# Attention then a feed-forward layer on one core: one ring of four PSUM banks, and a pair's steps dealt out anew

## The chip, the cores and the metric

One core of a Trainium2 chip runs the whole program. The core has a matrix engine (TensorE, rows PE; its weight loads PEld), VectorE (DVE), ScalarE (ACT), GpSimd (POOL), and SyncE (SP), which here issues the DMAs. Matmul results go to PSUM, eight banks of 128 partitions by 512 fp32 values. The metric is the device time of one execution in microseconds (us); the kernel before has a median of 1268.96 us over 3 runs (1266.4 to 1271.8).

## What is computed

Block-causal attention over 8 batches of 8 heads, 576 positions of width 64, in blocks of 64; its output, laid out as 4608 tokens of width 512, goes through a feed-forward layer (FFN) of inner width 2048:

```python
scores = (1 / sqrt(64)) * q @ k.T                  # per batch and head, 576 x 576
scores = where(block_i >= block_j, scores, -1e9)   # blocks of 64
attn   = softmax(scores)
x      = (attn @ v).transpose(0, 2, 1, 3).reshape(4608, 512)
h = x @ w_in                                       # 512 -> 2048
g = where(h >= 1, h, where(h <= -1, 0, (h + 1) ** 2 / 4))
out = g @ w_out                                    # 2048 -> 512
```

## The kernel before

**Pairs and steps.** Two heads of one batch make a pair; there are 32 pairs, run one after the other by `attention_steps`, a generator that hands out eight steps for each pair (called steps 0 to 7 below; a step ends at a `yield`). `cur` is the pair at work, `old` the one before it, `nxt` the one after. Batches from 2 on (pairs 8 to 31, flags `far` and `raw`) run their steps in one pattern, which is called the body below. `scores(j, g)` multiplies q and k of head j for one or two row tiles, reduces the maximum (DVE L505), takes exp (ACT L509, with a read of the accumulated sum behind it), and scales (DVE L491, L492, L515); a DMA then moves the result to another tile (prr). `turn(j, g)` transposes it on PE into a PSUM bank and `split` copies it out in a high part (ACT L545) and a low part (DVE L547). `turn_last` does the same for the last 64 rows of both heads, whose last 64 x 64 pieces, the corner, go by a fifth transposition to a bank and to the tiles pcs. `attn_v_first` multiplies the first 256 rows of both heads with v (8 matmuls, tiles pa), `attn_v(j)` the other 320 rows of one head (10 matmuls, tiles pb and pcs); `add_halves` adds the two halves (ACT L613 to xtmp, DVE L614 to x), and `store_x` makes x ready for the FFN. `turned_raw` (q and k of one head, four transpositions, L401) and `turned_last` (their last blocks, one transposition, L442) prepare the next pair: two copies on ACT (L388, L394) and two on DVE (L389, L395) that take turns on one bank, and in `turned_last` two more on DVE (L446).

**FFN.** `feed_forward` walks 9 chunks of 512 tokens and 16 slices of the inner width: `ffn_in` is 12 matmuls of 512 columns (L770, tile ph), then ACT L779, DVE L780, DVE L783, ACT L784 and POOL L785; `ffn_out` is 12 matmuls (L794, L799). From step 36 of the program on (pair 4) each step of attention is followed by one of them: in the body `ffn_in` follows steps 1, 3, 5, 7 and `ffn_out` steps 0, 2, 4, 6. What the FFN has left when attention ends, about 68 of its 288 pieces, runs alone.

**What sets the order.** The code is handed to a scheduler that orders each engine's instructions by the order in which they are written, but takes a later one first where its own clock says that an earlier one cannot start; it also gives each PSUM tile its bank. The engines then work through these fixed orders. A bank can be written again when its last reader is done, so a tile in a ring of three waits for the third or fourth one before it.

**Banks.** Before, attention has three banks (`ps_w`), `ffn_in` one of its own (`ps_h`), and `ffn_out` four (`ps_o`, lent to attention until the FFN starts):

```python
def work_bank(name):
    banks["n"] += 1
    if banks["free"] and banks["n"] % 2:
        return ps_o.tile([P, 512], F32, tag="po", name=name)
    return ps_w.tile([P, 512], F32, tag="work", name=name)
```

Of the kernel before, what the change touches and what calls it, by code (L numbers as in the profile page):

```python
# [23 lines left out]
def block_attn_then_ffn(  # L24
# [13 lines left out]
    P = 128  # L38
# [34 lines left out]
    dram = ctx.enter_context(tc.tile_pool(name="dram", bufs=1, space=bass.MemoryType.DRAM))  # L73
    ps_w = ctx.enter_context(tc.tile_pool(name="ps_w", bufs=3, space=bass.MemoryType.PSUM))
    ps_h = ctx.enter_context(tc.tile_pool(name="ps_h", bufs=1, space=bass.MemoryType.PSUM))
    ps_o = ctx.enter_context(tc.tile_pool(name="ps_o", bufs=NTT, space=bass.MemoryType.PSUM))

    banks = {"free": True, "n": 0}

    def work_bank(name):  # L80

        banks["n"] += 1
        if banks["free"] and banks["n"] % 2:
            return ps_o.tile([P, 512], F32, tag="po", name=name)
        return ps_w.tile([P, 512], F32, tag="work", name=name)
# [169 lines left out]
    class Pair:  # L255
# [238 lines left out]
        def scores(self, j, g):  # L494
            tiles = self.GROUPS[g]
            m = len(tiles)
            ps = work_bank("ps_s")
            pr = att3.tile([P, S], F32, tag="pr", name="pr")
            nm = small.tile([P, 2], F32, tag="nm", name="nm")
            sm = small.tile([P, 2], F32, tag="sm", name="sm")  # L500
            cols = [slice(at, at + (t + 1) * P) for t, at in tiles]
            for (t, _), cs in zip(tiles, cols):
                self.product(ps[:, cs], j, t * P, 0, (t + 1) * P, True, True)
            for i, cs in enumerate(cols):
                nc.vector.tensor_reduce(  # L505
                    out=nm[:, i : i + 1], in_=ps[:, cs], axis=AX.X, op=ALU.max, negate=True
                )
            for i, cs in enumerate(cols):
                nc.scalar.activation(  # L509
                    pr[:, cs], ps[:, cs], AF.Exp, bias=nm[:, i : i + 1], scale=1.0,  # L510
                    accum_out=sm[:, i : i + 1],
                )
            self.inverse(sm[:, :m])
            for i, cs in enumerate(cols):
                nc.vector.tensor_scalar_mul(pr[:, cs], pr[:, cs], sm[:, i : i + 1])  # L515
            self.pr[j, g] = as_float32r(pr[:, : cols[-1].stop], self.plain) if self.hop else [pr]

        def scores_last(self):
# [22 lines left out]
            nc.vector.tensor_scalar_mul(pr, pr, sm[:, 2:3])  # L541
            self.pr["last"] = as_float32r(pr, self.plain) if self.hop else [pr]

# [12 lines left out]
        def turn(self, j, g):  # L556
# [4 lines left out]
            for c0 in range(0, n, P):  # L561
                self.transposed(ps[:, c0 : c0 + P], pr, c0, P)
            if g == 0:
                self.split(ps[:, :n], *self.pa[j])
# [7 lines left out]
        def turn_last(self):  # L572
            pr = self.pr.pop("last")
            ps = work_bank("ps_t")
            for c0 in range(0, SM, P):
# [4 lines left out]
            )  # L580
            ps = work_bank("ps_t")
            self.transposed(ps[:BLK, :P], pr, SM, BLK)
            self.split(
                ps[:BLK, :P].rearrange("p (h c) -> p h c", h=2), *(x[:BLK] for x in self.pc)
            )

# [20 lines left out]

        def add_halves(self, ps, j, c0):
            main = slice(j * D, (j + 1) * D)
            rest = slice((1 - j) * D, (2 - j) * D)  # L610
            n = ps.shape[1]
            xtmp = att1.tile([P, G1], F32, tag="xtmp", name="xtmp")
            nc.scalar.copy(xtmp[main, :n], ps[rest, :])  # L613
# [17 lines left out]
        def attn_v_first(self):  # L631
# [3 lines left out]
            for j in range(2):  # L635
                self.weighted(ps[:, j * G0 : (j + 1) * G0], j, self.parts_first(j))
            for j in range(2):
                self.add_halves(ps[:, j * G0 : (j + 1) * G0], j, 0)

        def attn_v(self, j):  # L640
# [3 lines left out]
            self.weighted(ps, j, self.parts(j))  # L644
            self.add_halves(ps, j, G0)

# [16 lines left out]
    def attention_steps():  # L663
# [10 lines left out]
        for i, cur in enumerate(pairs + [None]):  # L674
# [9 lines left out]
            if far:  # L684
                old.attn_v_first()
            if near:
# [4 lines left out]
            if cur:  # L691
                cur.scores(0, 1)
                cur.turned_last()
            if i + 2 < len(pairs):
                pairs[i + 2].fetch()
            if near:
                old.attn_v(1)
                old.store_x()
            yield
            if far:  # L700
                old.attn_v(1)
                old.store_x()
            if not cur:
                return
            if cur.far:
                cur.scores(0, 2)
            else:
                cur.begin()
                cur.scores(0, 2)
                cur.turn(0, 0)  # L710
# [35 lines left out]
            else:  # L746
                cur.scores(1, 2)
                cur.attn_v(0)
                cur.turn(1, 0)
            yield  # L750
            if cur.far:
                cur.turn(1, 0)
                cur.attn_v(0)
            else:
                cur.turn(1, 1)
                cur.attn_v_first()
# [6 lines left out]
    def ffn_in(c, fc):  # L763
        at = (c * TCH) % RING
        ph = ps_h.tile([P, 512], F32, tag="ph", name="ph")
        fs = slice(fc * P, (fc + 1) * P)
# [118 lines left out]
```

## Time and profile before

| what | value |
|---|---|
| median of 3 runs | 1268.96 us (1266.4 to 1271.8) |
| the profiled execution: time | 1269.69 us |
| the profiled execution: span from first to last instruction | 1267.9 us |
| PE busy | 1200.1 us (95%) |
| DVE / ACT / POOL busy | 887.0 / 703.2 / 394.6 us |
| granted TensorE clock, mean | 0.981 |
| attention alone, weights prepared beside it | about the first 140 us |
| attention and FFN together | to about 1080 us |
| FFN alone | from about 1080 us |

A matmul's row gives its modelled end; matmuls overlap, so the distance from one start to the next says more than the length of a row. "[0.38 <-DVE x L614]" behind a row is the engine's idle time before it and what ended that idle time. In the rows of windows the columns are: the stretch, its length, then for PE, PEld, DVE, ACT and POOL the busy time with the count of instructions, then the granted TensorE clock, the share of the DMA engines' time, and GB/s.

### The profile page before, as it was taken

The numbers are of one execution on the slowest core, as the hardware profiler recorded it, in microseconds if no ns is written. First come the engines' busy times: TensorE is split into PE (matmuls) and PEld (weight loads), VectorE is DVE, ScalarE is ACT, GpSimd is POOL, SyncE is SP. The second block draws the span as 40 slices with busy tenths as digits, with TensorE's granted clock in tenths as the row PEclk, the third lists the DMA queues.
The fourth block names the chain that finished last, engine by engine and source line by source line (L and its number), as shares of the span: only waits on it lengthen the run. The fifth ranks groups of instructions, "written<-read, shape, count | busy, mean of one in ns | idle before, by whom it ended". The sixth has DMA issues, their size and how long they took to land.

```text
span 1267.9 us, 20253 instructions
## 1 busy us (share of the span) xinstructions
PE 1200.1 (95%) x6280; PEld 998.8 (79%) x6280; DVE 887.0 (70%) x2188; ACT 703.2 (55%) x1827; POOL 394.6 (31%) x430
## 2 busy tenths in 40 slices
PE   5888889899999999999999999999999999999998
PEld 4666667678888888888888888888888888888886
DVE  8898877758777777777777777787777777322222
ACT  5787656646566655665656655566556555222222
POOL 3555655522222222222222222222222222222222
PEclk9888988999999999999999999999999999999999
DMA  5566666667888655555554655465556433422432
GB/s 158 167 176 215 203 228 197 217 198 237 260 273 266 215 162 158 154 175 163 156 162 145 187 157 152 138 189 153 160 154 190 137 128 118 132 87 98 133 100 100
DMA packets 185259, 215.43 MB, mean 170 GB/s; under 512 B 113840, under 2 KB 132272, under 8 KB 184384
## 3 DMA queue, kind: packets, MB, share of 16 engines
q1 hardware_dynamic: 185152, 214.14, 54.9%
q8 instruction: 50, 0.82, 0.3%
q14 instruction: 57, 0.47, 0.1%
HBM read 134.74 MB, written 31.98 MB: 131 GB/s over the span
## 4 chain that ended last, share of the span: by engine, by line
PE 69%; DVE 16%; ACT 6%; issue 5%; DMA 1%; POOL 1%; SPq 1%; ACTq 0%; POOLq 0%; DVEq 0%
PE ph L770 29%; PE po L794 15%; PE po L799 7%; PE ps_av L591 7%; PE ps_s L482 4%; ACT pr L509 3%; PE ps_s L485 3%; DVE t L780 2%; PE ps_t L552 2%; DVE t L783 2%; ACT t L779 2%; DVE pb L547 2%; DVE nm L505 2%; DVE sm L491 1%; DVE pr L515 1%
## 5 line engine op out<-in xcount | busy, mean ns | idle before, releaser
L785 POOL TENSOR_TENSOR gl<-t,gh 128x512 fp32r<-128x512 f32 x144 | 187.5, 1302 | 510.2 <-ACT gh L784 333.2
L794 PE MATMUL po<-wo,gh 128*128 128x512 f32 x1152 | 296.1, 397 | 0.5 <-DMA wo<-wo_split 0.3
L794 PEld LDWEIGHTS po<-wo,gh 128*128 128x128 f32 x1152 | 212.5, 189 | 44.5 <-DMA wo<-wo_split 0.7
L770 PE MATMUL ph<-xh,wih 128*128 128x512 f32 x576 | 232.9, 404 | 1.6 <-DVE t L783 1.6
L770 PE MATMUL ph<-xh,wil 128*128 128x512 f32 x576 | 228.8, 397 | 0.0
L770 PE MATMUL ph<-xl,wih 128*128 128x512 f32 x576 | 227.8, 396 | 0.5 <-DVE xl L627 0.5
L780 DVE SCALAR_TENSOR_TENSOR t<-t 128x512 f32<-128x512 f32 x144 | 101.5, 705 | 168.0 <-ACT t L779 165.2
L779 ACT ACTIVATE t<-ph 128x512 f32<-128x512 f32 x144 | 85.9, 597 | 173.8 <-PE ph L770 173.8
L509 ACT ACTIVATE pr<-ps_s,nm 128x128 f32<-128x128 f32 (+3 forms) x256 | 134.1, 527 | 60.5 <-DVE nm L505 58.4
L784 ACT CAST gh<-t 128x512 fp32r<-128x512 f32 x144 | 89.5, 621 | 120.3 <-DVE t L783 120.0
L799 PE MATMUL po<-wo,gl 128*128 128x512 f32 x576 | 155.6, 392 | 0.0
L482 PE MATMUL ps_s<-ka,qa 68*128 68x288 f32 (+4 forms) x384 | 135.3, 367 | 15.0 <-ACT pr L509 5.4
L379 POOL TENSOR_TENSOR vsr<-vn,vsr 128x256 fp32r<-128x256 f32 (+1 forms) x96 | 55.2, 576 | 246.2 <-ACT vsr L378 244.6
L770 PEld LDWEIGHTS ph<-xh,wil 128*128 128x128 f32 x576 | 109.5, 190 | 23.8
L770 PEld LDWEIGHTS ph<-xh,wih 128*128 128x128 f32 x576 | 109.8, 191 | 21.7 <-DVE t L783 2.3
L799 PEld LDWEIGHTS po<-wo,gl 128*128 128x128 f32 x576 | 108.7, 189 | 23.1
L505 DVE TENSOR_REDUCE nm<-ps_s 128x1 f32<-128x128 f32 (+3 forms) x256 | 118.8, 482 | 10.4 <-PE ps_s L485 9.4
L770 PEld LDWEIGHTS ph<-xl,wih 128*128 128x128 f32 x576 | 109.7, 190 | 20.5 <-DVE xl L627 0.9
L485 PE MATMUL ps_s<-kb,qb 128*128 128x288 f32 (+4 forms) x384 | 121.1, 322 | 0.0
L515 DVE TENSOR_SCALAR pr<-pr,sm 128x128 f32<-128x128 f32 (+3 forms) x256 | 107.3, 440 | 5.4
L783 DVE TENSOR_TENSOR t<-ph,t 128x512 f32<-128x512 f32 x144 | 98.7, 686 | 2.2
L491 DVE TENSOR_SCALAR sm<-sm 128x1 f32<-128x1 f32 (+1 forms) x224 | 52.0, 232 | 68.3 <-ACT pr L509 65.7
(111 smaller groups left out, 1871.4 us busy)
## 6 DMA issues: line engine op xcount, KB each, us to landing
wo<-wo_split SPq DMA_DIRECT2D x144, 512.0 KB, 3.5
prr<-pr SPq DMA_DIRECT2D x96, 192.0 KB, 2.5
prr<-pr SPq DMA_DIRECT2D x72, 256.0 KB, 2.8
out_dram<-ob SPq DMA_DIRECT2D x36, 256.0 KB, 2.9
bits<-in_moe_w_in_dram SPq DMA_DIRECT2D x32, 256.0 KB, 3.5
bits<-in_moe_w_out_dram SPq DMA_DIRECT2D x32, 256.0 KB, 3.0
wo_split<-ws SPq DMA_DIRECT2D x16, 512.0 KB, 2.9
qa<-qb SPq DMA_DIRECT2D x63, 128.0 KB, 2.4
```

The costliest lines, as they stand in the source:

```text
L482: nc.tensor.matmul(ps, qa[:KA, j, c0 : c0 + P], ka[:KA, j, k0 : k0 + n], start=first, stop=False)
L485: nc.tensor.matmul(ps, qb[:, j, c0 : c0 + P], kb[:, j, k0 : k0 + n], start=False, stop=last)
L505: nc.vector.tensor_reduce(out=nm[:, i : i + 1], in_=ps[:, cs], axis=AX.X, op=ALU.max, negate=True)
L509: nc.scalar.activation(pr[:, cs], ps[:, cs], AF.Exp, bias=nm[:, i : i + 1], scale=1.0, accum_out=sm[:, i : i + 1],)
L515: nc.vector.tensor_scalar_mul(pr[:, cs], pr[:, cs], sm[:, i : i + 1])
L770: nc.tensor.matmul(ph, w[:, cc, fs], x[:, cc, xs], start=(cc == 0 and i == 0), stop=(cc == NCC - 1 and i == 2),)
L779: nc.scalar.activation(t_, ph, AF.Relu, bias=0.5, scale=0.5)
L780: nc.vector.scalar_tensor_tensor(out=t_, in0=t_, scalar=1.0, in1=t_, op0=ALU.min, op1=ALU.mult)
L783: nc.vector.tensor_tensor(out=t_, in0=ph, in1=t_, op=ALU.max)
L785: nc.gpsimd.tensor_tensor(out=gl, in0=t_, in1=gh.bitcast(F32), op=ALU.subtract)
L794: nc.tensor.matmul(po[tt], gh[:, ts_], wo[:, w, :], start=(fc == 0 and w == 0), stop=False)
L799: nc.tensor.matmul(po[tt], gl[:, ts_], wo[:, 0, :], start=False, stop=fc == NFC - 1)
```

## The change

- `ps_h` is gone; `ps_w` has four banks instead of three, and `ffn_in` takes its bank from the same ring as attention.
- In the body `attn_v(0)` of the old pair moves from step 7 to step 0, `attn_v_first` from step 0 to step 1, and `attn_v(1)` in step 2 behind `scores(0, 2)` instead of ahead of it.
- `turned_last` for the next pair moves from its own step 1 to step 6 of the pair ahead of it.
- The corner is no longer transposed in `turn_last` (step 6) into a bank of its own, but in `turn(1, 0)` (step 7) into the unused last quarter of that bank.
- `add_halves` gets its xtmp from its caller; `attn_v_first` uses one for both heads. `moved` only gives a name to a line.

```diff
-    ps_w = ctx.enter_context(tc.tile_pool(name="ps_w", bufs=3, space=bass.MemoryType.PSUM))
-    ps_h = ctx.enter_context(tc.tile_pool(name="ps_h", bufs=1, space=bass.MemoryType.PSUM))
+    ps_w = ctx.enter_context(tc.tile_pool(name="ps_w", bufs=4, space=bass.MemoryType.PSUM))
...
@@ turn
             for c0 in range(0, n, P):
                 self.transposed(ps[:, c0 : c0 + P], pr, c0, P)
+            if self.far and j == 1 and g == 0:
+                self.turn_corner(self.pr.pop(("last",)), ps[:BLK, n : n + P])
...
@@ turn_last
-            ps = work_bank("ps_t")
-            self.transposed(ps[:BLK, :P], pr, SM, BLK)
-            self.split(
-                ps[:BLK, :P].rearrange("p (h c) -> p h c", h=2), *(x[:BLK] for x in self.pc)
-            )
+            if not self.far:
+                self.turn_corner(pr, work_bank("ps_t")[:BLK, :P])
+
+        def turn_corner(self, pr, ps):
+
+            self.transposed(ps, pr, SM, BLK)
+            self.split(ps.rearrange("p (h c) -> p h c", h=2), *(x[:BLK] for x in self.pc))
...
@@ attn_v_first
+            xtmp = att1.tile([P, G1], F32, tag="xtmp", name="xtmp")
             for j in range(2):
-                self.add_halves(ps[:, j * G0 : (j + 1) * G0], j, 0)
+                self.add_halves(ps[:, j * G0 : (j + 1) * G0], j, 0, xtmp)
...
@@ attention_steps, step 0
             if far:
-                old.attn_v_first()
+                old.attn_v(0)
@@ step 1
             if cur:
                 cur.scores(0, 1)
-                cur.turned_last()
+                if not cur.raw:
+                    cur.turned_last()
...
+            if far:
+                old.attn_v_first()
@@ step 2
-            if far:
-                old.attn_v(1)
-                old.store_x()
-            if not cur:
-                return
-            if cur.far:
-                cur.scores(0, 2)
-            else:
-                cur.begin()
-                cur.scores(0, 2)
+            if not cur:
+                old.attn_v(1)
+                old.store_x()
+                return
+            if not cur.far:
+                cur.begin()
+            cur.scores(0, 2)
+            if far:
+                old.attn_v(1)
+                old.store_x()
+            if not cur.far:
                 cur.turn(0, 0)
@@ step 6
+            if nxt and nxt.raw:
+                nxt.turned_last()
@@ step 7
             if cur.far:
                 cur.turn(1, 0)
-                cur.attn_v(0)
@@ ffn_in
-        ph = ps_h.tile([P, 512], F32, tag="ph", name="ph")
+        ph = work_bank("ph")
```

**PE in the body, steps 6 and 7**, from `turn(0, 2)` to the first matmul of `ffn_in`. Before (ps_t: the transposed tiles; ps_s: the scores; po: `ffn_out`; ps_av: attn times v; ps_qk: the next pair's q and k):

```order
L552 MATMUL ps_t<-ident_r,prr 128x128 x4
L552 MATMUL ps_t<-ident_r,prr 64x128
L482 MATMUL ps_s<-ka,qa 128x512
L485 MATMUL ps_s<-kb,qb 128x512
L794 MATMUL po<-wo,gh 128x512 x8
L799 MATMUL po<-wo,gl 128x512 x4
L552 MATMUL ps_t<-ident_r,prr 128x128 x3
```

The ten matmuls of `attn_v(0)` follow here, then four transpositions for ps_qk (L401) and `ffn_in`. The change:

```order
L558 MATMUL ps_t<-ident_r,prr 128x128 x4
L482 MATMUL ps_s<-ka,qa 128x512
L485 MATMUL ps_s<-kb,qb 128x512
L442 MATMUL ps_qk<-ident_r,qk 128x128
L809 MATMUL po<-wo,gh 128x512 x8
L814 MATMUL po<-wo,gl 128x512 x4
L558 MATMUL ps_t<-ident_r,prr 128x128 x3
L558 MATMUL ps_t<-ident_r,prr 64x128
L401 MATMUL ps_qk<-ident_r,qk 128x128 x4
L785 MATMUL ph<-xh,wih 128x512
```

The corner (64x128) moved behind `ffn_out`, the transposition of `turned_last` (L442) came in behind the scores, and between the corner and `ffn_in` only four transpositions are left. In every fourth pair the scheduler puts four of the po matmuls ahead of L442, and three of the next step's po matmuls ahead of that step's transpositions. The bank that this `ffn_in` takes is that of the 512-column scores in the same piece; the bank of the ten matmuls of `attn_v(0)`, now in step 0, is that of the L401 transpositions.

**DVE in the body, steps 6 and 7**, from the reduction of the 512-column scores to L395 of `turned_raw`. Before:

```order
L505 TENSOR_REDUCE nm<-ps_s 128x1
L491 TENSOR_SCALAR sm<-sm 128x1
L492 RECIPROCAL sm<-sm 128x1
L515 TENSOR_SCALAR pr<-pr,sm 128x512
L547 TENSOR_TENSOR pa_8700<-ps_t,pa_8699 128x384
L614 TENSOR_TENSOR x_8703<-ps_av,xtmp 64x320
L389 SCALAR_TENSOR_TENSOR qb<-ps_qk,qb 64x512
L395 TENSOR_TENSOR kb<-ps_qk,kb 64x512
```

The change:

```order
L505 TENSOR_REDUCE nm<-ps_s 128x1
L389 SCALAR_TENSOR_TENSOR qb<-ps_qk,qb 64x2x64
L491 TENSOR_SCALAR sm<-sm 128x1
L395 TENSOR_TENSOR kb<-ps_qk,kb 64x2x64
L492 RECIPROCAL sm<-sm 128x1
L446 TENSOR_SCALAR qa<-ps_qk 64x2x64
L515 TENSOR_SCALAR pr<-pr,sm 128x512
L446 TENSOR_SCALAR ka<-ps_qk 64x2x64
L553 TENSOR_TENSOR pcs_107<-ps_t,pcs_106 64x128
L389 SCALAR_TENSOR_TENSOR qb<-ps_qk,qb 64x512
L553 TENSOR_TENSOR pa_8671<-ps_t,pa_8670 128x384
L395 TENSOR_TENSOR kb<-ps_qk,kb 64x512
```

The four copies of `turned_last` (the 64x2x64 ones) came in between the reduction and the scaling, the corner's low part (pcs) moved from ahead of the reduction to behind it, and the addition of `attn_v(0)` (L614) went to step 0.

**PE early, in pair 1**, around the transpositions for q of the next pair. Before, two of the first `ffn_in`'s twelve matmuls stand here, long before their place in the code (the other ten follow in pairs 1 to 4):

```order
L422 MATMUL ps_qk<-ident_r,qs 128x128 x4
L770 MATMUL ph<-xh,wih 128x512
L770 MATMUL ph<-xl,wih 128x512
L554 MATMUL ps_t<-ident_r,pr 128x128 x4
L482 MATMUL ps_s<-ka,qa 128x384
L485 MATMUL ps_s<-kb,qb 128x384
```

The change:

```order
L422 MATMUL ps_qk<-ident_r,qs 128x128 x4
L560 MATMUL ps_t<-ident_r,pr 128x128 x4
L482 MATMUL ps_s<-ka,qa 128x384
L485 MATMUL ps_s<-kb,qb 128x384
L560 MATMUL ps_t<-ident_r,pr 128x128 x4
L560 MATMUL ps_t<-ident_r,pr 64x128
```

With the bank of its own gone, all twelve matmuls of the first `ffn_in` stand in pair 4, at their place in the code.

More of the change, by code (lines that the diff above doesn't have):

```diff
@@ L515, in scores, with moved @@
                 nc.vector.tensor_scalar_mul(pr[:, cs], pr[:, cs], sm[:, i : i + 1])
-            self.pr[j, g] = as_float32r(pr[:, : cols[-1].stop], self.plain) if self.hop else [pr]
+            self.pr[j, g] = [pr[:, : cols[-1].stop]]
+            self.moved(j, g)
+        def moved(self, *key):
+            if self.hop:
+                self.pr[key] = as_float32r(self.pr[key][0], self.plain)
         def scores_last(self):
@@ L541, in scores_last @@
             nc.vector.tensor_scalar_mul(pr, pr, sm[:, 2:3])
-            self.pr["last"] = as_float32r(pr, self.plain) if self.hop else [pr]
+            self.pr["last",] = [pr]
+            self.moved("last")
         def split(self, ps, hi, lo=None):
@@ L572, in turn_last @@
         def turn_last(self):
-            pr = self.pr.pop("last")
+            pr = self.pr["last",] if self.far else self.pr.pop(("last",))
             ps = work_bank("ps_t")
@@ L606, in parts, with add_halves @@
             return (*parts, (NTL, SM - G0, [x[:, j, :] for x in self.pc]))
-        def add_halves(self, ps, j, c0):
+        def add_halves(self, ps, j, c0, xtmp):
             main = slice(j * D, (j + 1) * D)
@@ L611, in add_halves @@
             n = ps.shape[1]
-            xtmp = att1.tile([P, G1], F32, tag="xtmp", name="xtmp")
             nc.scalar.copy(xtmp[main, :n], ps[rest, :])
@@ L644, in attn_v @@
             self.weighted(ps, j, self.parts(j))
-            self.add_halves(ps, j, G0)
+            self.add_halves(ps, j, G0, att1.tile([P, G1], F32, tag="xtmp", name="xtmp"))
         def store_x(self):
```

## The prediction

> **What bounds the kernel now.** First I read the view of windows, one stretch for each stage (attention with the preparation of weights, the transition, the body, the FFN alone):
>
> ```profile
> 40.00:140.00 100.00, 81.95 (x437) 65.22 (x436) 91.47 (x261) 77.17 (x232) 55.90 (x69) 0.90 0.62 187
> 140.00:280.00 140.00, 123.48 (x570) 95.51 (x568) 99.59 (x246) 79.27 (x221) 68.90 (x84) 0.91 0.67 213
> 280.00:1080.00 800.00, 785.88 (x4353) 665.98 (x4353) 613.70 (x1506) 477.01 (x1227) 210.46 (x219) 1.00 0.58 175
> 1080.00:1268.00 188.00, 182.79 (x807) 150.64 (x805) 49.89 (x73) 44.27 (x74) 43.99 (x34) 0.99 0.33 108
> ```
>
> Up to 140 us VectorE is the busy one (91.5 of 100 us). From 280 us on the matrix engine is: 785.9 of 800 us, at a granted clock of 1.00. The body is all that the new steps touch, and PE's idle time there is 14.1 us. Then the waits of PE in that stretch (engine and line, what it waited for, us in total, times, longest):
>
> ```profile
> PE ps_qk L442 <- DVE x L614: 8.9, 23, 0.4
> PE ps_s L482 <- ACT pr L509: 5.2, 17, 0.3
> ```
>
> These two are the 14.1 us. The first stands in step 1 of 23 pairs: the transposition of `turned_last` wants the bank that `attn_v_first` used, and the second addition is late. The second stands in step 6 of 17 pairs: the 512-column scores want the bank of the 384-column scores of step 5, whose exp is late. Both are one delay: PE is ahead of VectorE and ScalarE, and a ring of three banks passes it on.
>
> The idle time understates them, since a matmul's row runs on while nothing follows. From start to start, in one pair:
>
> ```profile
> 595.08 0.34 PE L485 MATMUL ps_s<-kb,qb 128*128 128x384 f32 x1
> 595.26 0.39 PE L770 MATMUL ph<-xh,wih 128*128 128x512 f32 x1
> ...
> 611.83 0.34 PE L485 MATMUL ps_s<-kb,qb 128*128 128x384 f32 x1
> 612.55 0.25 PE L442 MATMUL ps_qk<-ident_r,qk 128*128 128x128 f32 x1 [0.38 <-DVE x L614]
> 612.64 0.46 PE L770 MATMUL ph<-xh,wih 128*128 128x512 f32 x1
> ```
>
> Where nothing is waited for, the next start comes 0.18 us after the 384-column matmul; here it comes 0.72 us after. The stall is 0.54 us, not 0.38. (The Trainium skill, "Trainium Kernel Development and Optimization", Performance Expectations, says that matmul busy time is a bad metric because matmuls are pipelined; by the busy time the two stalls would be worth 14.1 us, by the starts some 20, and the starts here bear the page out.)
>
> **The stretch in which the pair's second half is decided.** Steps 6, 7 and the next step 0, from the timeline of the same pair:
>
> ```profile
> 597.99 0.51 PE L552 MATMUL ps_t<-ident_r,prr 128*128 128x128 f32 x5
> 598.58 0.19 ACT L509 ACTIVATION_READ_ACCUMULATOR pr<-ps_s,nm 128x1 f32 x1
> 598.82 0.50 PE L482 MATMUL ps_s<-ka,qa 68*128 68x512 f32 x1 [0.33 <-ACT pr L509]
> 599.40 0.39 PE L794 MATMUL po<-wo,gh 128*128 128x512 f32 x1
> 600.73 0.68 DVE L783 TENSOR_TENSOR t<-ph,t 128x512 f32<-128x512 f32 x1
> 601.33 0.27 DVE L547 TENSOR_TENSOR pcs<-ps_t,pcs 64x128 fp32r<-64x128 f32 x1
> 601.52 0.67 DVE L505 TENSOR_REDUCE nm<-ps_s 128x1 f32<-128x512 f32 x1
> 602.14 0.37 PE L552 MATMUL ps_t<-ident_r,prr 128*128 128x128 f32 x3
> 602.28 0.69 ACT L509 ACTIVATE pr<-ps_s,nm 128x512 f32<-128x512 f32 x1 [0.22 <-DVE nm L505]
> 602.35 1.31 PE L591 MATMUL ps_av<-pb,vsr 128*128 128x320 f32 x8
> 602.87 0.19 ACT L509 ACTIVATION_READ_ACCUMULATOR pr<-ps_s,nm 128x1 f32 x1
> 603.09 0.15 DVE L491 TENSOR_SCALAR sm<-sm 128x1 f32<-128x1 f32 x1 [0.90 <-ACT pr L509]
> 603.28 0.16 DVE L492 RECIPROCAL sm<-sm 128x1 f32<-128x1 f32 x1
> 603.48 0.49 DVE L515 TENSOR_SCALAR pr<-pr,sm 128x512 f32<-128x512 f32 x1
> 603.66 0.53 PE L401 MATMUL ps_qk<-ident_r,qk 128*128 128x128 f32 x4
> 603.88 0.55 DVE L547 TENSOR_TENSOR pa<-ps_t,pa 128x384 fp32r<-128x384 f32 x1
> 604.03 0.46 PE L770 MATMUL ph<-xh,wih 128*128 128x512 f32 x1
> 606.87 0.37 PE L552 MATMUL ps_t<-ident_r,prr 128*128 128x128 f32 x3
> 607.08 0.29 PE L482 MATMUL ps_s<-ka,qa 68*128 68x128 f32 x1
> 607.61 1.03 PE L591 MATMUL ps_av<-pa,vsr 128*128 128x256 f32 x8
> ```
>
> Three transpositions take 0.21 us (602.14 to 602.35), so five take 0.35 and the scores could start at 598.34; they start at 598.82, 0.05 after the accumulator's read ends (598.77). That stall is 0.48 us. A pair with both loses 1.02 us.
>
> **What the change does, part by part.** No instruction is added or taken away; every matmul, copy and DMA has its old size. No DMA belongs to a moved step; on SP's queue only the loads of q and k for a later pair begin earlier, after L401 in step 7 instead of after L442 in step 1, and nothing reads them for a pair's time.
>
> *Step 1's stall goes.* L442 leaves step 1. `attn_v_first` comes in there, but with half a step of matmuls and `ffn_in` behind it; the bank of its sums is not asked for again before step 3. Gain 0.54 us a pair.
>
> *Step 6's stall goes.* The 512-column scores take the bank of the transpositions of step 5, whose low copy is long done. L442 now takes the bank of the 384-column scores, free for PE at 598.82. PE comes there at 597.99 + 0.28 (four transpositions) + 0.58 (598.82 to 599.40) = 598.85. Gain 0.48 us, with 0.03 us to spare; if the exp were 0.2 us later, L442 would wait 0.17.
>
> *A stall in step 7 comes.* I follow PE on: L442 takes 0.09 (612.55 to 612.64), to 598.94; `ffn_out` 2.74 (599.40 to 602.14), to 601.68; four transpositions 0.28, to 601.96; L401 0.37 (603.66 to 604.03), to 602.33. The ten matmuls of `attn_v(0)`, 1.31 us long, are no longer in between. There `ffn_in` wants the bank of the 512-column scores. Their reduction is behind DVE L783, which this change leaves where it was; without the corner's copy it starts at 601.33 instead of 601.52 and ends 0.67 later at 602.00. The exp follows after 0.09 (as 602.19 to 602.28) and its accumulator read ends 0.78 after its start (602.28 to 603.06), at 602.87; PE goes on 0.05 later, at 602.92. Stall 0.59 us. Queued behind it: all of `ffn_in`, then step 0.
>
> *A stall in step 0 comes.* PE goes on: `ffn_in` 2.84 (604.03 to 606.87), to 605.76; three transpositions and four matmuls of scores 0.74 (606.87 to 607.61), to 606.50. There `attn_v(0)` now wants the bank of L401, whose last reader is DVE L395. VectorE has the new pieces ahead of it; these rows give them and the pair of L389 and L395:
>
> ```profile
> 605.08 0.69 DVE L389 SCALAR_TENSOR_TENSOR qb<-ps_qk,qb 64x512 fp32r<-64x512 f32 x1 [0.21 <-ACT qb L388]
> 605.80 0.58 ACT L394 CAST kb<-ps_qk 64x512 fp32r<-64x512 f32 x1 [0.75 <-DVE qb L389]
> 606.42 0.69 DVE L395 TENSOR_TENSOR kb<-ps_qk,kb 64x512 fp32r<-64x512 f32 x1 [0.65 <-ACT kb L394]
> ...
> 615.36 0.29 DVE L395 TENSOR_TENSOR kb<-ps_qk,kb 64x128 fp32r<-64x128 f32 x1
> 615.66 0.28 DVE L446 TENSOR_SCALAR qa<-ps_qk 64x128 fp32r<-64x128 f32 x1
> 615.96 0.29 DVE L446 TENSOR_SCALAR ka<-ps_qk 64x128 fp32r<-64x128 f32 x1
> ```
>
> From the accumulator read (602.87) L491 starts at 602.90; by distances from start to start: L491 0.19, L395 of the last blocks 0.30, L492 0.20, L446 0.30, L515 0.40 (603.48 to 603.88), L446 0.30, pcs 0.19 (601.33 to 601.52). L389 starts at 604.78 and ends at 605.47; ACT L394 runs 605.50 to 606.08, DVE L395 606.12 to 606.81, and PE may go at 606.86. Stall 0.36 us. In that stretch pa's low copy ends at about 605.95, just as PE wants that bank (605.97): nothing by itself, and anything up to 0.36 us would only come out of the wait behind it.
>
> *The fourth bank* adds nothing to that: `ffn_in` takes one of the four in turn, and the new waits are at banks three to five tiles back.
>
> *Every fourth pair.* Three `ffn_out` matmuls (0.69 us by 2.74 / 12 each) stand ahead of step 0's transpositions there and cover its 0.36; step 7's 0.59 stays. These are the 6 pairs of 23 without the second wait before.
>
> *The early part.* The first `ffn_in` no longer fills gaps in pairs 1 to 4. It costs nothing if PE's idle time near pair 4 takes it in (16.5 us of 140 in that stretch), and 2.84 us if none of it does. I take half, 1.4.
>
> **Sum.** Before: 17 x 1.02 + 6 x 0.54 = 20.6 us. After: 17 x (0.59 + 0.36) + 6 x 0.59 = 19.7 us. Gain 0.9, less 1.4: 0.5 us slower than the profiled execution's 1269.69 us (span 1267.9), so 1270.2. The median of the runs shown is 0.7 us lower, which gives **1269 us**: the stalls change place, not size.
>
> **How sure the two new stalls are.** Before shows neither. Below: both zero, if VectorE gets to the reduction before L783, or skips over its waits. Above: the chain of a dozen small instructions is put together from rows of other places; the same rows show waits of 0.2 to 0.7 us between engines that share a bank, so 0.35 us more a pair is possible (8 us).
>
> **Rivals.**
>
> *Faster: one or both new stalls don't come.* For it: PE waits 0.59 us at one place only, and a reduction 0.6 us earlier would free it. Against it: DVE's order has L783 ahead, and L783 waits for ScalarE after step 5's `ffn_in`. Without step 0's stall: 1269 - 17 x 0.36 = 1263. Without both: 1269 - 19.7 = 1249.
>
> *Slower: the copies of `turned_last` are the chain.* In step 1 they had slack; now L389, L395 and two L446 stand between the exp and L395 of `turned_raw`, and four readers take turns on the bank of the corner and `turn(1, 0)`. From 0.27 us a pair beyond my sum (23 x 0.27 = 6.3 us) the kernel is measurably slower; at 0.6 us it is 1269 + 13.8 = 1283. Against it: distances are measured, and only their order is new.
>
> *Slower: the early part.* Without the early matmuls PE is idle more where the granted clock is already 0.90 and 0.91. If the whole 2.84 us were lost (1.4 us more than I take) and the granted clock fell by another 0.05 over the first stretch's 100 us (5 us), it would be 1269 + 1.4 + 5 = 1275. The Trainium skill, "TensorE: Matmul & The Clock Gate", Part 1 (The HAM clock gate), has the clock at half rate after an idle window of about 3.4 us; the rows' 0.90 beside idle PE and 1.00 in the full body agree. By that page one more such window would cost an estimated 1.7 us.
>
> **How the numbers follow.** About 0.5% (6.3 us) is what a measurement can tell from no change. Stalls change place (1263 to 1275): 0.50, all within. Fewer stalls (1249 to 1263): 0.29, all faster. Longer chain (1276 to 1283): 0.15, all slower. Early part: 0.06, two thirds slower. So faster 0.29, same 0.52, slower 0.19. The likeliest case's own range is 1263 to 1275; to leave out no more than 2 in 10, 1250 to 1281.
>
> **What would show it.** In the body's waits: L442 and the scores gone; `ffn_in` waiting for ACT L509 some 23 times, 0.4 to 0.6 us each, and ps_av for DVE L395 some 17 times. PE idle in the body stays near 14 us. The prediction is wrong if `ffn_in` in step 7 starts within 0.1 us of L401's end, or if PE's idle time in the body halves or doubles.

## The result, and the profile after

The change makes the kernel 0.6% slower: 1274.92 us, median of 12 runs (1272.94 to 1277.37), against 1267.57 us for the kernel before (12 runs, 1264.21 to 1271.8); the ratio is 1.006, interval 1.0048 to 1.0071. That is 7.4 us. The forecast was 1269 us and no measurable change.

The view of windows of the kernel after, the same stretches as before; the first two are the early part, the third is the body:

```profile
40.00:140.00 100.00, 77.40 (x415) 63.72 (x413) 86.06 (x248) 73.29 (x219) 51.20 (x66) 0.85 0.62 186
140.00:280.00 140.00, 123.62 (x585) 96.48 (x586) 108.55 (x257) 82.91 (x234) 73.69 (x87) 0.94 0.67 213
280.00:1080.00 800.00, 784.61 (x4322) 661.34 (x4321) 617.33 (x1500) 473.39 (x1222) 209.42 (x218) 1.00 0.58 175
```

PE's busy time in the body is 784.6 us, 1.3 less than before; the busy time hardly tells what happened. The waits of PE in the body have changed places:

```profile
PE ph L785 <- ACT pr L509: 6.5, 17, 0.4
PE ps_s L482 <- PE ps_t L558: 4.4, 17, 0.3
PE ps_t L558 <- DMA prr<-pr: 2.3, 5, 0.6
```

L442 and the 512-column scores wait no more. `ffn_in` waits for the exp in step 7, and a new row has the scores of step 0 wait, by the profile for PE itself. How long a pair is shows best from the first 288-column scores of step 3 to the same matmul of the next pair. Before:

```profile
620.23 0.37 PE L482 MATMUL ps_s<-ka,qa 68*128 68x288 f32 x1
...
653.72 0.36 PE L482 MATMUL ps_s<-ka,qa 68*128 68x288 f32 x1
```

and after:

```profile
623.21 0.36 PE L482 MATMUL ps_s<-ka,qa 68*128 68x288 f32 x1
...
656.98 0.36 PE L482 MATMUL ps_s<-ka,qa 68*128 68x288 f32 x1
```

An ordinary pair grew from 33.49 to 33.77 us; every fourth one stayed about where it was (33.2 to 33.3 before, 33.05 to 33.4 after). At the first pair of the body the kernel after is 0.8 us behind, at the last one 6.3, at the end 6.2 (of two profiled executions whose times, 1269.69 and 1275.87 us, are as far apart). The loss grows over the whole body.

Steps 6 and 7 and the next step 0 of an ordinary pair, from the timeline of the kernel after:

```profile
600.91 0.47 PE L482 MATMUL ps_s<-ka,qa 68*128 68x512 f32 x1
601.49 0.28 PE L442 MATMUL ps_qk<-ident_r,qk 128*128 128x128 f32 x1
603.99 0.68 DVE L505 TENSOR_REDUCE nm<-ps_s 128x1 f32<-128x512 f32 x1
604.69 0.50 PE L401 MATMUL ps_qk<-ident_r,qk 128*128 128x128 f32 x4
604.76 0.69 ACT L509 ACTIVATE pr<-ps_s,nm 128x512 f32<-128x512 f32 x1
605.34 0.19 ACT L509 ACTIVATION_READ_ACCUMULATOR pr<-ps_s,nm 128x1 f32 x1
605.57 0.15 DVE L491 TENSOR_SCALAR sm<-sm 128x1 f32<-128x1 f32 x1 [0.58 <-ACT pr L509]
605.59 0.50 PE L785 MATMUL ph<-xh,wih 128*128 128x512 f32 x1 [0.40 <-ACT pr L509]
605.85 0.29 DVE L395 TENSOR_TENSOR kb<-ps_qk,kb 64x128 fp32r<-64x128 f32 x1
607.08 0.29 DVE L446 TENSOR_SCALAR ka<-ps_qk 64x128 fp32r<-64x128 f32 x1
607.40 0.28 DVE L553 TENSOR_TENSOR pcs<-ps_t,pcs 64x128 fp32r<-64x128 f32 x1
607.72 0.68 DVE L389 SCALAR_TENSOR_TENSOR qb<-ps_qk,qb 64x512 fp32r<-64x512 f32 x1
607.72 0.48 ACT L551 CAST pa<-ps_t 128x384 fp32r<-128x384 f32 x1 [1.12 <-DVE pcs L553]
608.43 0.56 DVE L553 TENSOR_TENSOR pa<-ps_t,pa 128x384 fp32r<-128x384 f32 x1
608.46 0.38 PE L558 MATMUL ps_t<-ident_r,prr 128*128 128x128 f32 x3
609.05 0.69 DVE L395 TENSOR_TENSOR kb<-ps_qk,kb 64x512 fp32r<-64x512 f32 x1
609.09 0.30 PE L482 MATMUL ps_s<-ka,qa 68*128 68x128 f32 x1 [0.26 <-PE ps_t L558]
609.89 1.32 PE L601 MATMUL ps_av<-pb,vsr 128*128 128x320 f32 x8
```

Step 7: L401 takes 0.37 us, so `ffn_in` could start at 605.06; it starts at 605.59, 0.06 after the accumulator's read ends (605.53). Step 0: three transpositions take 0.21 us, so the scores could start at 608.67; they start at 609.09, 0.10 after VectorE's low copy of pa ends (608.99). And `attn_v(0)`, 0.53 us of scores later (0.74 less 0.21), could start at 609.62 and starts at 609.89, 0.15 after L395 ends (609.74). So step 0's stall has two parts, 0.42 and 0.27, and both hang on one VectorE chain that runs from L491 to L395 with gaps of at most 0.13 us. The profile names neither releaser ("PE ps_t L558", nothing for L601): the ends of the DVE rows have to be laid beside PE's starts. The order of the ring says the same: the scores take the bank of `turn(1, 0)`, whose last reader is pa's low copy, and `attn_v(0)` takes that of L401, whose last reader is L395. (ACT's copy L394 ends at 609.01, close to the start of the scores too, but it reads the bank of L401.)

Before its copy of pa ACT sits idle for 1.12 us, and it starts 0.04 us after VectorE's copy of the corner ends, although the two read different columns: since the change they lie in one bank. The Trainium skill, "PSUM — Partial Sum Buffer", section "PSUM bank collisions raise a hardware error", says that ScalarE and VectorE may not be in one bank and quadrant at once, whichever columns they read, and that the compiler keeps them apart; this row agrees.

**All stalls of the body.** The table has, for the two kernels and those of the next section, what one profiled execution of each shows. The stalls are summed from start to start over 280 to 1080 us (what a distance exceeds the one without a wait by, where that is over 0.15 us; worked out from all PE rows of each trace, and uncertain by about 1 us through the choice of the distance without a wait). "Begins" is the start of the first 288-column scores of pair 8, "body" the time from there to the same matmul of pair 31, 23 pairs later. The median is that of all runs.

| kernel | stalls in the body, us | begins, us | body, us | body less stalls | median, us |
|---|---|---|---|---|---|
| before | 21.1 | 286.2 | 768.6 | 747.5 | 1267.6 |
| after | 26.5 | 287.0 | 774.1 | 747.6 | 1274.9 |
| A, ring alone | 20.6 | 286.3 | 766.8 | 746.2 | 1268.7 |
| B, steps alone | 27.0 | 281.5 | 775.4 | 748.4 | 1274.6 |
| C, without L446's copies | 15.3 | 289.0 | 763.4 | 748.1 | 1266.0 |
| D, turned_last in step 2 | 12.2 | 286.0 | 756.9 | 744.7 | 1259.1 |
| E, attn_v(0) back | 36.6 | 287.1 | 784.4 | 747.8 | 1283.9 |
| F, D and E | 9.5 | 284.4 | 755.6 | 746.1 | 1255.5 |
| G, D without the ring | 9.8 | 281.6 | 757.9 | 748.1 | 1255.9 |
| H, F without the ring | 7.6 | 282.4 | 754.2 | 746.6 | 1252.9 |
| I, before, turned_last in step 2 | 29.9 | 280.1 | 776.6 | 746.7 | 1275.9 |
| J, before, step 2 turned round | 21.3 | 284.6 | 769.1 | 747.8 | 1267.5 |
| K, I and J | 9.2 | 284.1 | 755.2 | 746.0 | 1254.3 |
| L, after, step 2 turned back | 26.6 | 287.2 | 773.9 | 747.3 | 1273.8 |

The body's length spans 30 us, and less its stalls not quite 4: what these kernels differ by in the body is their stalls. From pair 31's mark to the end all of them take 213.0 to 214.3 us. What is left of their differences lies ahead of the body, where the seven kernels with the ring (after, A, C, D, E, F, L) come to pair 8 at 286.7 us on average, the seven others at 282.9.

### The profile page after: what moved, and what is told of

Its sections match the earlier page's. It is cut to its first block, busy times and chain, and to the rows that moved or that the text cites. A ratio compares the mean times of both kernels' runs of the same rounds, so it can differ in the third digit from the quotient of the medians.

```text
span 1274.1 us, 20178 instructions
## 1 busy us (share of the span) xinstructions
PE 1199.9 (94%) x6280; PEld 998.5 (78%) x6280; DVE 898.3 (71%) x2188; ACT 701.8 (55%) x1827; POOL 394.9 (31%) x430
## 4 chain that ended last, share of the span: by engine, by line
PE 66%; DVE 16%; ACT 7%; DMA 4%; issue 3%; POOL 1%; SPq 1%; ACTq 0%; POOLq 0%; DVEq 0%
PE ph L785 25%; PE po L809 14%; PE ps_av L601 9%; PE po L814 7%; PE ps_s L482 4%; PE ps_s L485 3%; ACT pr L509 3%; PE ps_t L558 2%; DVE pb L553 2%; DVE nm L505 2%; DVE t L795 2%; DVE pr L515 2%; DVE t L798 2%; DMA prr<-pr 2%; DVE sm L491 1%
## 5 line engine op out<-in xcount | busy, mean ns | idle before, releaser
L800 POOL TENSOR_TENSOR gl<-t,gh 128x512 fp32r<-128x512 f32 x144 | 192.0, 1333 | 617.8 <-ACT gh L799 230.9
L809 PE MATMUL po<-wo,gh 128*128 128x512 f32 x1152 | 299.3, 400 | 0.5 <-DMA wo<-wo_split 0.3
L809 PEld LDWEIGHTS po<-wo,gh 128*128 128x128 f32 x1152 | 208.0, 188 | 40.9 <-DMA wo<-wo_split 0.8
L482 PE MATMUL ps_s<-ka,qa 68*128 68x288 f32 (+4 forms) x384 | 132.2, 359 | 13.2 <-PE ps_t L558 4.4
L515 DVE TENSOR_SCALAR pr<-pr,sm 128x128 f32<-128x128 f32 (+3 forms) x256 | 118.7, 484 | 4.7
L379 POOL TENSOR_TENSOR vsr<-vn,vsr 128x256 fp32r<-128x256 f32 (+1 forms) x96 | 50.8, 530 | 147.9 <-ACT vsr L378 147.7
L482 PEld LDWEIGHTS ps_s<-ka,qa 68*128 68x128 f32 x384 | 74.7, 194 | 20.3 <-PE ps_t L558 6.5
```

The costliest lines, as they stand in the source:

```text
L482: nc.tensor.matmul(ps, qa[:KA, j, c0 : c0 + P], ka[:KA, j, k0 : k0 + n], start=first, stop=False)
L800: nc.gpsimd.tensor_tensor(out=gl, in0=t_, in1=gh.bitcast(F32), op=ALU.subtract)
L809: nc.tensor.matmul(po[tt], gh[:, ts_], wo[:, w, :], start=(fc == 0 and w == 0), stop=False)
```

## The experiments

Each kernel ran 4 to 12 times, beside runs of the kernel before on the same chip; the ratios are to those, and the medians of different experiments come from different chips.

**A. The ring alone**: the kernel before with four banks for both.

```diff
-    ps_w = ctx.enter_context(tc.tile_pool(name="ps_w", bufs=3, space=bass.MemoryType.PSUM))
-    ps_h = ctx.enter_context(tc.tile_pool(name="ps_h", bufs=1, space=bass.MemoryType.PSUM))
+    ps_w = ctx.enter_context(tc.tile_pool(name="ps_w", bufs=4, space=bass.MemoryType.PSUM))
...
-        ph = ps_h.tile([P, 512], F32, tag="ph", name="ph")
+        ph = work_bank("ph")
```

> The steps of before, with the change's ring of four banks alone; the early part is then the change's too. Theory chain (the change loses because turned_last's copies on VectorE stand between the exp of step 6 and attn*v of step 0): little moves, 1267 (1263 to 1270). Step 1's wait passes from L442 to the ffn_in behind it (the bank of attn_v_first, about 0.45 us instead of 0.54), step 6's wait of 0.48 us stays. Theory ring (ffn_in loses by sharing the ring): slower, 1273 or more, with ffn_in waiting for exp in step 7. Theory early (the loss is in the first 280 us, where the first ffn_in is no longer a filler): 1273 to 1275.

Measured 1268.72 us, ratio 0.9998 (0.9986 to 1.001). Its waits in the body are those of before:

```profile
PE ph L769 <- DVE x L613: 8.2, 23, 0.6
PE ps_s L481 <- ACT pr L508: 6.2, 17, 0.6
```

Only the matmul that meets the wait has moved by one piece, from L442 to `ffn_in` behind it. The ring, with the first `ffn_in`'s changed place in the early part, changes nothing measurable in the whole time. That may be two small effects that cancel: the body is 1.8 us shorter than before's, and the kernels with the ring are later at its beginning (table).

**B. The steps alone**: the change with the banks of before (the diff of A turned round).

> The change's steps with the banks of before (three for attention, one for ffn_in); the early part is that of before. Theory chain: the body is as slow as the change's, 0.25 to 0.35 us a pair over before, 1272 to 1274. Theories ring and early: as before, 1267 to 1268.

Measured 1274.63 us, ratio 1.0045 (1.0028 to 1.0063), against 1.006 (1.0048 to 1.0071) for the change: by these intervals most or all of the loss is the steps'. Its first waits:

```profile
PE ps_qk L402 <- ACT pr L510: 7.4, 17, 0.5
PE ps_t L559 <- DMA prr<-pr: 2.7, 3, 1.5
PE ps_s L483 <- PE ps_t L559: 1.8, 11, 0.2
```

The exp of step 6's scores stops `turned_raw` instead of `ffn_in`, and step 0 waits as in the change.

**C. Without the two L446 copies**: for raw pairs the last blocks of q and k aren't copied to their other half, so the last rows of attention are another computation; the chain is two instructions shorter.

```diff
-                for i, a in enumerate((qa, ka)):
-                    nc.vector.tensor_scalar_mul(
-                        last_blocks(a)[:D], ps[i * D : (i + 1) * D], 1.0 if i else SCALE
-                    )
                 return
```

> The change without the two VectorE copies (L446) of turned_last for the raw pairs, 0.3 us each; q's and k's last blocks are then not filled in their first half, so the last rows of the attention are another computation. Theory chain: what VectorE saves comes out of step 0's waits (0.71 us to 0.1 or 0.2 a pair): 1263 to 1267. Theories ring and early: no more than 1 us, 1274.

Measured 1265.98 us, ratio 0.9977 (0.9962 to 0.9993), 8.9 us below the change. Step 0 in its timeline (its line numbers are four lower):

```profile
605.00 0.56 DVE L549 TENSOR_TENSOR pa<-ps_t,pa 128x384 fp32r<-128x384 f32 x1
605.62 0.69 DVE L395 TENSOR_TENSOR kb<-ps_qk,kb 64x512 fp32r<-64x512 f32 x1
605.90 0.29 PE L478 MATMUL ps_s<-ka,qa 68*128 68x128 f32 x1
606.46 1.32 PE L597 MATMUL ps_av<-pb,vsr 128*128 128x320 f32 x8
```

L395 now ends at 606.31, before PE is there, and step 0's stall is gone, while step 7's stands (its `ffn_in` starts 0.89 us behind L401). Two copies of 0.3 us were worth step 0's 0.69 us in an ordinary pair, and the body is 10.7 us shorter: the wait is VectorE's chain, as the rival in the prediction had it.

**D. turned_last in step 2**: the change with the last blocks' transposition and its copies at the head of the pair's own step 2 instead of step 6 of the pair ahead.

```diff
@@ step 2
+            if cur.raw:
+                cur.turned_last()
             cur.scores(0, 2)
@@ step 6
-            if nxt and nxt.raw:
-                nxt.turned_last()
```

> The change with turned_last moved from step 6 of the pair ahead to the head of the pair's own step 2, where VectorE has room. Theory chain: step 0's two waits (0.45 and 0.26 us) go or shrink to 0.3, and nothing takes their place, so at most 0.85 us a pair remains and at least 1261; if the bank that ffn_in gets in step 7 is another too, about 1252 (1248 to 1258). Theory ring: step 7's wait stays and little else moves, 1268 to 1275. Theory early: 1273 to 1275.

Measured 1259.07 us, ratio 0.993 (0.991 to 0.995): faster than both kernels, and between the two figures expected (at least 1261; 1248 to 1258). Steps 7 and 0:

```profile
597.77 0.25 PE L401 MATMUL ps_qk<-ident_r,qk 128*128 128x128 f32 x1
597.85 0.47 PE L785 MATMUL ph<-xh,wih 128*128 128x512 f32 x1
598.39 0.19 ACT L509 ACTIVATION_READ_ACCUMULATOR pr<-ps_s,nm 128x1 f32 x1
598.76 0.28 DVE L553 TENSOR_TENSOR pcs<-ps_t,pcs 64x128 fp32r<-64x128 f32 x1
600.39 0.56 DVE L553 TENSOR_TENSOR pa<-ps_t,pa 128x384 fp32r<-128x384 f32 x1
601.01 0.69 DVE L395 TENSOR_TENSOR kb<-ps_qk,kb 64x512 fp32r<-64x512 f32 x1
601.05 0.30 PE L482 MATMUL ps_s<-ka,qa 68*128 68x128 f32 x1
601.85 1.32 PE L601 MATMUL ps_av<-pb,vsr 128*128 128x320 f32 x8
```

Step 7's stall is gone: `ffn_in` starts 0.08 behind L401's last matmul. By the order of the ring, without a tile for L442 in step 6 it falls on the bank of `turn_last`, whose copies are long done. The corner's low copy starts 0.18 us after the accumulator's read ends (598.58), against 1.87 us in the change (605.53 to 607.40). Step 0 keeps 0.43 us, still behind pa's low copy (0.10) and L395 (0.15). By the starts the change loses 0.55 + 0.69 us here and D 0.43: 17 x 0.81 is 13.8 of the 15.8 us between them.

**E. attn_v(0) back in step 7**, attn_v_first back in step 0, the rest as the change.

```diff
@@ step 0
-                old.attn_v(0)
+                old.attn_v_first()
@@ step 1
-                old.attn_v_first()
@@ step 7
                 cur.turn(1, 0)
+                cur.attn_v(0)
```

> The change, with attn_v(0) back in step 7 and attn_v_first back in step 0. Theory order of PE: the change's two waits come because PE reaches ffn_in of step 7 and the scores of the next step 0 earlier by the ten matmuls of attn_v(0), 1.31 us; with them back both waits (0.55 us in step 7, 0.7 us in step 0) are covered: 1274.9 - 17 x 1.25 - 6 x 0.55 = 1250 us; up to 1256 if the last blocks' transposition in step 6, which had 0.03 us to spare, now waits some 0.3 us a pair. Theory place of turned_last: its copies in step 6 delay VectorE whatever PE does; part of the wait stays and it is 1262 us or more.

Measured 1283.91 us, ratio 1.0136 (1.0121 to 1.0151): by far slower than both theories had it. Neither had asked what `attn_v(0)` reads. Its waits and the place:

```profile
PE ps_av L601 <- DVE pcs L553: 22.1, 23, 1.0
```

```profile
610.39 0.19 ACT L509 ACTIVATION_READ_ACCUMULATOR pr<-ps_s,nm 128x1 f32 x1
612.45 0.28 DVE L553 TENSOR_TENSOR pcs<-ps_t,pcs 64x128 fp32r<-64x128 f32 x1
612.78 0.30 PE L601 MATMUL ps_av<-pcs,vsr 128*128 128x64 f32 x1 [1.00 <-DVE pcs L553]
```

The last matmul of `attn_v(0)` multiplies the low part of the corner, which the change transposes only in step 7, and whose copy VectorE reaches 1.87 us after the accumulator's read ends, behind the copies of `turned_last`. So three of the change's moves hang together: with the corner and `turned_last` where the change puts them, `attn_v(0)` has to leave step 7.

**F. D and E together**: turned_last in step 2, attn_v(0) in step 7.

> The change with turned_last in step 2 of its own pair, and attn_v(0) and attn_v_first where they were before. With turned_last in step 2 alone the trace shows 0.43 us of stall a pair, in step 0 (the scores behind pa's low copy, then attn_v(0) behind L395); with attn_v(0) ahead of it in step 7 PE comes there 1.31 us later and the stall should go: 1259 - 17 x 0.43 = 1252 us (1249 to 1255). If VectorE's work a pair sets the pace, the stall only appears elsewhere: 1257 to 1261 us.

Measured 1255.52 us, ratio 0.9906 (0.9891 to 0.9921). The move that costs the change 9 us (E) costs nothing on D and seems to gain some 3 us, though the intervals of the two ratios still overlap: with the copies of `turned_last` away, the corner's low copy starts 0.18 us after the accumulator's read and not 1.87. The time lies between the two ranges expected. The trace shows that step 0's stall went and most of it came back elsewhere, as the second theory had it:

```profile
597.72 0.28 DVE L553 TENSOR_TENSOR pcs<-ps_t,pcs 64x128 fp32r<-64x128 f32 x1
597.74 0.61 PE L601 MATMUL ps_av<-pcs,vsr 128*128 128x64 f32 x2
```

The two matmuls of `attn_v(0)` with the corner take 0.61 us together, where the same two take 0.33 us in `attn_v(1)`, which waits for nothing: the second one waits for the corner's low copy, which ends at 598.00. From start to start that is 0.3 us in each of 23 pairs, 7.2 of the 9.5 us of stalls that are left; in the body the gain on D is 1.3 us.

**G. D with the banks of before.**

> The change with turned_last in step 2 of its own pair, on the banks of before (three and ffn_in's own). Theory banks don't matter: no tile then asks for a bank whose reader is late but in step 0, as in the ring: 1259 us, 1256 to 1262. Theory the ring is what the gain with turned_last in step 2 needs (a bank less for attention puts the waits for the exp back): 1265 us or more.

Measured 1255.88 us, ratio 0.991 (0.9893 to 0.9926): the gain needs no ring. The body is 1.0 us longer than D's, so what the median gains on D lies ahead of the body.

**H. F with the banks of before.**

> The change with turned_last in step 2, attn_v(0) and attn_v_first where they were, and the banks of before. Each of the two (attn_v(0) back, banks back) gave 1255.5 to 1255.9 us where turned_last in step 2 alone gave 1259.1. If they add, since one takes a stall of 0.43 us a pair and the other only the first ffn_in's place in the early part: 1252 us (1250 to 1254). If both are the same few us: 1255 to 1257 us.

Measured 1252.87 us, ratio 0.989 (0.9874 to 0.9906), the fastest of all. The medians add up as the first case had it; by the ratios each of the two gains alone is not clear of noise against D, both together are. In its body PE is busy 797.4 of 800 us.

**I. The kernel before, with turned_last in step 2** and nothing else.

```diff
@@ step 1
-                cur.turned_last()
+                if not cur.raw:
+                    cur.turned_last()
@@ step 2
+            if cur and cur.raw:
+                cur.turned_last()
             if far:
                 old.attn_v(1)
```

> The kernel before with one thing moved: turned_last of raw pairs from behind scores(0, 1) in step 1 to the head of step 2. Theory each stall stands by itself: step 1's stall of 0.54 us in 23 pairs goes, step 6's 0.48 us in 17 pairs stays: 1268.2 - 12.4 = 1256 us. Theory VectorE's and ScalarE's pace sets the pair: PE, earlier by 0.54 us, waits longer in step 6, and it stays within 1264 to 1269 us.

Measured 1275.89 us, ratio 1.007 (1.0049 to 1.0092): slower, which neither theory had. Its waits, and the part of its timeline in step 2:

```profile
PE ps_s L482 <- ACT pr L509: 16.8, 40, 0.6
```

```profile
615.17 0.48 PE L482 MATMUL ps_s<-ka,qa 68*128 68x512 f32 x1
616.47 0.29 DVE L395 TENSOR_TENSOR kb<-ps_qk,kb 64x128 fp32r<-64x128 f32 x1
617.40 0.49 DVE L614 TENSOR_TENSOR x<-ps_av,xtmp 64x320 f32<-64x320 f32 x1
617.92 0.69 DVE L505 TENSOR_REDUCE nm<-ps_s 128x1 f32<-128x512 f32 x1
```

The scores stand behind `turned_last` and `attn_v(1)` on PE, and so does their reduction on VectorE: the reduction starts 2.75 us after the scores. Every exp behind it in the pair is late, and PE waits for one in steps 3, 5 and 6.

**J. The kernel before, with scores(0, 2) ahead of attn_v(1) in step 2** and nothing else.

```diff
@@ step 2, far pairs
+                cur.scores(0, 2)
                 old.attn_v(1)
                 old.store_x()
-                cur.scores(0, 2)
```

> The kernel before with scores(0, 2) in step 2 ahead of attn_v(1) and nothing else. Theory swap: step 6's wait for the exp (0.48 us in 17 pairs) goes, step 1's for the second addition (0.54 us in 23) stays: 1268 - 8 = 1260 us. Theory both moves are needed (the wait of step 1 sets VectorE's place): 1266 to 1270 us.

Measured 1267.48 us, ratio 0.9999 (0.9986 to 1.0011): nothing by itself. Both stalls of before are there, 12.6 and 8.0 us.

**K. I and J together.**

> The kernel before with two things moved: turned_last of raw pairs to the head of step 2, and scores(0, 2) in step 2 ahead of attn_v(1). The kernel with the first move alone waited in steps 3, 5 and 6 for the exp (1.40 us in one ordinary pair, 1275.9 us). Theory swap: the scores of step 2 reach VectorE 1.31 us earlier, and every reduction and exp behind them in the pair with them: these waits go, 1253 to 1258 us. Theory corner or attn_v: the gain with turned_last in step 2 came from the change's other moves; it stays above 1268 us.

Measured 1254.28 us, ratio 0.99 (0.9884 to 0.9916). The same place in its timeline:

```profile
608.00 0.45 PE L482 MATMUL ps_s<-ka,qa 68*128 68x512 f32 x1
608.72 0.69 DVE L505 TENSOR_REDUCE nm<-ps_s 128x1 f32<-128x512 f32 x1 [0.38 <-PE ps_s L485]
```

The reduction starts 0.72 us after the scores instead of 2.75, and the copies of `turned_last` come behind it. The waits of steps 3 and 5 are gone but for single ones, and so is step 1's of before, 12.7 us over 23 pairs. Step 6's stays, against the expectation:

```profile
PE ps_s L482 <- ACT pr L509: 5.4, 18, 0.3
```

One move alone costs 8 us, the other alone nothing, both together bring 13. Of the change this kernel has only the turned order in step 2, and `turned_last` stands in another place than there; with the banks and all else as before it has 13.4 of the 14.8 us that the fastest kernel here gains.

**L. The change with attn_v(1) back ahead of scores(0, 2)** (the diff of J turned round, in the change).

> The change with attn_v(1) in step 2 back ahead of scores(0, 2). Theory swap: the scores of step 2 come 1.31 us later to VectorE, which is the late one in steps 6 to 0: slower than the change, 1280 us or more. Theory only the chain of steps 6 to 0 counts: it follows the exp of step 6's scores, the earlier scores are long done: 1273 to 1277 us, as the change.

Measured 1273.75 us, ratio 1.0058 (1.004 to 1.0075), within 1.2 us of the change: where `turned_last` isn't in step 2, the order there is worth nothing.

## Why the prediction was right in its range and wrong in its sum

- **The number**: the measured 1274.92 us lies inside 1263 to 1275 by less than 0.1 us, and that is luck. The range was made for stalls that change place and not size; they grew, and a loss clear of noise came where none was forecast.
- **What bounds the kernel**: right. PE with its stalls is the time in all fourteen kernels, and counting from start to start rather than by busy time was needed (20.6 us forecast for before, 21.1 by the whole trace).
- **Step 1's and step 6's stalls go**: right, both rows are gone. L442 in step 6 had been given 0.03 us to spare; in the pair shown it starts 0.05 us after the accumulator's read ends, and by the starts it waits 0.03 us at most.
- **Step 7's stall, 0.59 us**: right in place and cause, 0.53 us in the pair shown, 9.5 us over 17 pairs. Wrong was that it comes in the 6 other pairs too. Those lose instead some 0.6 us to the DMA of prr (5 times) and 0.2 at L442 (6 times), 4.3 us in all against 3.5 forecast.
- **Step 0's stall, 0.36 us: the step that failed.** The mechanism was right (`attn_v(0)` behind L395 of `turned_raw`, behind the copies of `turned_last`); its size came out at 0.69 us, so this is the term of the sum that was too small. Laid on the end of the accumulator's read, the chain was forecast to bring L395 to its start at 608.78 on the clock of the trace after; it starts at 609.05. Of these 0.27 us, 0.15 had come by the start of pcs, where the small copies stand 0.3 us or more apart; 0.13 come from pcs to L389, 0.32 us where a distance of 0.19 from another place had been taken. Another 0.10 is PE, which started 0.15 us after L395's end and not 0.05. With 0.04 for PE coming later, 0.37 - 0.04 = 0.33 us is just the difference of 0.69 and 0.36. Over 17 pairs that is 5.6 us. C shows the cause: take 0.6 us out of the chain and the stall goes. D shows it with nothing left out: where the copies of `turned_last` stand elsewhere, 0.43 us are left, although PE, without step 7's stall, comes earlier there.
- **pa's low copy costs nothing by itself**: right; the scores did wait for it, 0.42 us, but as had been said, that comes out of the wait for L395 behind it; the total is set by L395.
- **The early part, 1.4 us**: borne out in its sign, its size is uncertain. The seven profiled executions with the ring come to pair 8 at 284.4 to 289.0 us, the seven without at 280.1 to 286.2; the granted clock from 40 to 140 us is 0.83 to 0.86 in the first and 0.88 to 0.93 in the others. The means are 3.8 us apart, but single executions of one kernel differ by some microseconds (before's profiled one was 2.1 us slower than its median), so an estimate from these figures is 2 to 4 us. Of the 7.4 us by which the medians differ the body makes 5.5 and the end nothing, which leaves about 2 for the early part. Whether the first `ffn_in`'s place does it or the other order of the banks is open.
- **The sum**: forecast was a body 0.9 us better; by the stalls it is 26.5 - 21.1 = 5.4 us worse, by its length 5.5.
- **The rivals**: the longer chain of the copies of `turned_last` is what happened. It had been given 0.15, on the ground that the distances were measured and only their order new. The bound stated beside it ("0.35 us more a pair is possible") was almost exactly what came. And the likeliest case's range, 1263 to 1275, was counted as all within; 1274.9 lies in it and yet beyond the 0.5%, since the median of before came out at 1267.6. The rival of the early part saw one thing rightly: the granted clock of the first stretch fell by the 0.05 it names (0.90 to 0.85). But in the next stretch it rose from 0.91 to 0.94, and of the 5 us it was priced at the two profiles show 0.8 at pair 8.
- **The signs named**: PE's idle time in the body stayed near 14 us (15.4) while the kernel lost 7.4, so that sign could not have shown the loss. `ffn_in` waited for ACT 17 times and not 23, and the row of ps_av for DVE L395 does not exist, since the profile names no releaser there.

What the prediction did not see at all: that `turned_last` had a better place, in step 2 of its own pair, and that its worth there depends on the order in step 2 (I, J, K).

## What to carry to other kernels

In this kernel one engine is full and the others follow close behind. There a moved piece of work was paid by the longest chain of small instructions that it lengthened, not by its own cost: find the instruction on the follower's queue that releases the next bank, and ask what now stands ahead of it. Moves interact: one cost 8 us alone, another nothing, both together gained 13, so a dealt-out order should be tried piece by piece and in pairs before it is judged. A chain put together from distances measured elsewhere misses the differences between neighbours; here ten distances came out 0.27 us short of 3.5. And a single execution can differ from the median by 2 or 3 us, so the time between two fixed marks inside one trace (here pair 8 and pair 31) says more about one stretch than the whole time does.

## What was not expected of the hardware

- The releaser that the profile names can be missing: two waits of 0.42 and 0.27 us a pair stood under "PE ps_t L558" and under nothing, while PE started 0.10 and 0.15 us after the ends of DVE L553 and L395, in the change and in D alike. That these two are the releasers is worked out from the order of the ring. After ACT's accumulator read it started 0.06 us behind. The Trainium skill, "Perfetto Trace Analysis", section "Per-instruction lifecycle: what the profiler-reported window actually captures", has the semaphore travel after the reported end of a DVE or ACT instruction; these gaps agree, and give its order of size here.
- ACT and DVE, which read different columns of one bank, took turns: ACT waited 25.0 us over 24 times in the body (1.12 us in the pair shown), since the corner shares the bank of pa.
- Waits of PE for the DMA of prr appeared in the body, where before has none: 2.3 us over 5 times in the change, and up to 1.5 us at once in B. What sets them was not tried.
